# Half-row products of three pairs side by side, and output products ahead of two pairs, in a fused attention and feed-forward kernel

## The chip, the cores and the metric

The kernel runs on one core of a Trainium2 chip. The metric is the device time of one execution in microseconds (us). A program on one core has its runs called fast unless one is over 1.5% above the fastest of the same kernel; all comparisons of times below are between fast runs. The engines are named as in the profile: PE is TensorE (PEld its weight loads), ACT is ScalarE, DVE is VectorE, SP issues the DMAs.

## The reference, cut to what matters

```python
xn = layernorm(x)                              # x: 1 x 2048 x 448
q, k, v = split(xn @ wqkv)                     # 16 heads of 28
logits = q . k[pos - 2*j], j = 0..7            # window of 8, dilation 2, scaled, masked
s = softmax(logits) @ v[...] @ wo
h = gelu(xn @ w1 + b1)                         # 448 -> 1792
g = silu(h @ w2 + b2)                          # 1792 -> 448
out = x + s * g
```

The depth of the first products is 448 = 3 x 128 + 64. The last 64 rows, the "rest", fill half of the TensorE array, so the rests of two products run side by side in its two halves: a pass of two rests takes 0.22 us, as one full product does. The passage of TensorE from full rows to rests, or back, is called a crossing below.

## The kernel before

The sequence is handled in four blocks of 512 positions. Each block has a feed-forward stage with seven pairs of 128-wide tiles (`k` = 0 to 6), and then (but for the last block) units of attention, each with scores `S`, exponentials `E` and value product `psO`. PSUM has two pools: psA with two tiles of two banks each (tag "A"), shared by the scores and most pairs, and psB with four one-bank tiles, for everything else. The kernel fixes the order of the instructions on each engine itself (`manual_schedule`).

```python
def ffn1_tiles(k):
    if k in (0, 3):
        return [psB.tile([P, CH], F32, name="ps_h", tag="B") for _ in range(2)]
    ps = psA.tile([P, 2, CH], F32, name="ps_h", tag="A")
    return [ps[:, i, :] for i in range(2)]
# ffn1_full: per half three 128-row products; ffn1_rest: two 64-row products side by side
def ffn1(c, k, even):
    ps = ffn1_tiles(k)
    if even: ffn1_full(c, k, ps, True);  ffn1_rest(c, k, ps, False)
    else:    ffn1_rest(c, k, ps, True);  ffn1_full(c, k, ps, False)
    return ps

def feed_forward_1(c, ps, wos):
    nc.scalar.preload_act_table_set(SET_GELU)
    gelu(0, ps)
    for k in range(1, MT // 2):
        if (c, k) in ((0, 6), (1, 4), (2, 4)):
            qk_pair(c + 1, 0, True, DD)                # a q/k pair of the next block
        odd = k in {0: (1, 3, 5, 6), 3: (1, 3, 5)}.get(c, (1, 3, 4, 6))
        ps = ffn1(c, k, not odd)
        gelu(k, ps)
        # ... norm statistics behind pairs 1 and 3
        if k in ((3, 5, 6) if c == 3 else (4,)):
            # ... wo_job: four products with wo into psB, gated by g, added to x
        if c and k in (3, 5):
            silu_job(4 * (c - 1) + k - 3)              # tanh on ScalarE, gate g on VectorE
            silu_job(4 * (c - 1) + k - 2)
    nc.scalar.preload_act_table_set(SET_EXP)
```

Pairs with the rest last and pairs with the rest first alternate, so rests already lie in twos.

The softmax here doesn't subtract the row's maximum and nothing guards it: scores larger than these inputs give would overflow.

Of the kernel before, what the change touches and what calls it, by code (L numbers as in the profile page):

```python
# [16 lines left out]
P = 128  # L17
NT = S // P
NC = 4
# [14 lines left out]
def kernel(  # L34
# [58 lines left out]
    def xt(t):  # L93
        return x_sb[t // 4][:, t % 4, :]
# [99 lines left out]
    def qk_full(c, g, ps, first, copies):  # L194
        for w in range(2):
            for kt in range(3):
                nc.tensor.matmul(ps[w][:, :], wqk[:, kt, 16 * w + 4 * g:16 * w + 4 * g + 4, :],  # L197
                                 xnT[:, kt, LEAD + c * CH:LEAD + (c + 1) * CH],
                                 start=(first and kt == 0), stop=(not first and kt == 2))
            if not first:  # L200
                qk_put(c, g, w, ps, copies)

    def qk_rest(c, g, ps, first, copies):

        for w in range(2):
            r = slice(64 * w, 64 * w + 64)
            nc.tensor.matmul(ps[w][:, :], wqk[r, 3, 16 * w + 4 * g:16 * w + 4 * g + 4, :],  # L207
                             xnT[r, 3, LEAD + c * CH:LEAD + (c + 1) * CH], start=first, stop=not first)
        if not first:
            for w in range(2):  # L210
                qk_put(c, g, w, ps, copies)

# [3 lines left out]
    def qk_pair(c, g, even, copies):  # L216

        ps = [psB.tile([P, CH], F32, name="ps_qk", tag="B") for _ in range(2)]
        for f in ((qk_full, qk_rest), (qk_rest, qk_full))[not even]:
            f(c, g, ps, f is (qk_full, qk_rest)[not even], copies)  # L220
# [3 lines left out]
    def v_mm(b):  # L224
        ps = psB.tile([P, D], F32, name="ps_v", tag="B")
        o = LEAD + QB * b - 7
        for kt in range(KT):
            nc.tensor.matmul(ps[:, :], xnT[:, kt, o:o + P], wv[:, kt, :],  # L228
                             start=(kt == 0), stop=(kt == KT - 1))
        return ps  # L230
# [8 lines left out]
    def ffn1_tiles(k):  # L239
        if k in (0, 3):  # L240
            return [psB.tile([P, CH], F32, name="ps_h", tag="B") for _ in range(2)]
        ps = psA.tile([P, 2, CH], F32, name="ps_h", tag="A")
        return [ps[:, i, :] for i in range(2)]

    def ffn1_full(c, k, ps, first):
        for i in range(2):
            m = 2 * k + i
            for kt in range(3):
                nc.tensor.matmul(ps[i][:, :], w1[:, kt, m * P:(m + 1) * P],  # L249
                                 xnT[:, kt, LEAD + c * CH:LEAD + (c + 1) * CH],  # L250
                                 start=(first and kt == 0), stop=(not first and kt == 2))

    def ffn1_rest(c, k, ps, first):

        for i in range(2):
            m = 2 * k + i
            r = slice(64 * i, 64 * i + 64)
            nc.tensor.matmul(ps[i][:, :], w1[r, 3, m * P:(m + 1) * P],  # L258
                             xnT[r, 3, LEAD + c * CH:LEAD + (c + 1) * CH], start=first, stop=not first)

    def gelu(k, ps):
        for i in range(2):
            m = 2 * k + i
            nc.scalar.activation(hT[:, m, :], ps[i][:, :], ACT.Gelu_apprx_tanh, bias=b1f[:, m:m + 1])  # L264

    def ffn1(c, k, even):

        ps = ffn1_tiles(k)
        if even:
            ffn1_full(c, k, ps, True)  # L270
            ffn1_rest(c, k, ps, False)
        else:
            ffn1_rest(c, k, ps, True)
            ffn1_full(c, k, ps, False)
        return ps
# [59 lines left out]
    def wo_put(t, ps, cs=slice(0, D)):  # L335
        sg = work.tile([P, D], BF16, name="sg", tag="sg", bufs=3)
        nc.vector.scalar_tensor_tensor(out=sg[:, cs], in0=ps[:, 0:cs.stop - cs.start], scalar=0.5, in1=g_sb[t % NG][:, cs],  # L337
                                       op0=ALU.mult, op1=ALU.mult)
        o_t = work.tile([P, D], BF16, name="o_t", tag="o_t", bufs=3)
        nc.vector.tensor_tensor(out=o_t[:, cs], in0=xt(t)[:, cs], in1=sg[:, cs], op=ALU.add)  # L340
        nc.sync.dma_start(dram_rows(out_par, t, 1)[:, 0, cs], o_t[:, cs])
# [49 lines left out]
    def feed_forward_1(c, ps, wos):  # L391

        nc.scalar.preload_act_table_set(SET_GELU)
        gelu(0, ps)
        for k in range(1, MT // 2):
            if (c, k) in ((0, 6), (1, 4), (2, 4)):

                qk_pair(c + 1, 0, True, DD)
            odd = k in {0: (1, 3, 5, 6), 3: (1, 3, 5)}.get(c, (1, 3, 4, 6))
            ps = ffn1(c, k, not odd)  # L400
            gelu(k, ps)
            if c + 2 < NC and k in (1, 3):
                for t in range(4 * c + 7 + k, 4 * c + 9 + k):
                    ln_stats(t)
            if k in ((3, 5, 6) if c == 3 else (4,)):
                for _ in range(4 if c == 2 else 2):
                    if wos:
                        wo_job(wos.pop(0))
            if c and k in (3, 5):
                silu_job(4 * (c - 1) + k - 3)  # L410
                silu_job(4 * (c - 1) + k - 2)
        nc.scalar.preload_act_table_set(SET_EXP)


    with tc.manual_schedule(engines={ENG.PE, ENG.Activation, ENG.DVE, ENG.Pool, ENG.SP}):
        nc.scalar.preload_act_table_set(SET_EXP)
        busy(9)
# [16 lines left out]
        v_put(0, v0)  # L434
        ln_apply(2)
        pT.append(ln_tr(2))
        v1 = v_mm(1)
        ln_put(2, pT[2])
        v_put(1, v1)
# [3 lines left out]
        ln_put(3, pT[3])  # L443
        v_put(2, v2)
        v_job(3)
        pb = psB.tile([P, MT], BF16, name="pb", tag="B")
        nc.tensor.transpose(pb[:, :], b1r[:, :], ident[0:MT, 0:MT])
# [4 lines left out]
        late_constants()  # L452
        nc.vector.tensor_copy(b1f[:], pb[:, :])
        for g in range(4):
            qk_pair(0, g, g % 2 == 0, DA)
            if g == 3:
                ln_stats(7)
                ln_rstd(4, 4)
            else:
                ln_stats(4 + g)  # L460
        ps = ffn1(0, 0, True)
        for t in range(4, 8):
            ln_apply(t)
            ln_dma(t)
        late_loads()

        units = iter(range(NB))
        for c in range(3):
            feed_forward_1(c, ps, [[], [0, 1], [2, 3, 4, 5]][c])
            n = c + 1  # L470
            qk_pair(n, 1, True, DD)
            norm = lambda: None
            vs = iter(range(4 * n, 4 * n + (5 if c == 2 else 4)))
            for i in range(5):
                b = next(units)
                if i == 0:
                    tail = []
                    E = qk_unit(b, lambda: qk_pair(n, 2, False, (nc.vector.tensor_copy, lambda *a: tail.append(a))))
                    if n + 1 < NC:
                        ln_rstd(4 * n + 4, 4)  # L480
                    nc.scalar.copy(*tail[0])
                    qk_pair(n, 3, True, DA)
                else:
                    E = qk_unit(b)
# [70 lines left out]
```

## Time and profile before

| | before |
|---|---|
| time, median | 167.58 us (167.44 to 167.74, 3 runs) |
| span of the profiled run | 165.6 us |
| TensorE busy | 158.9 us, 96% |
| ScalarE busy | 125.9 us, 76% |
| VectorE busy | 112.9 us, 68% |

The prediction below shows the lines to read. A view that it doesn't show is the list of what TensorE waited for, with the total, the number and the longest, in us. Before the change, apart from the start of the kernel, it holds nothing but two short entries without a releaser, which come from lost records:

```profile
PE ps_qk L197 <- issue: 0.2, 1, 0.2
PE ps_h L249 <- issue: 0.2, 1, 0.2
```

Waits inside a merged row (the scores' 0.28 us) don't appear there; they are seen as a row that lasts longer than its like.

### The profile page before, as it was taken

Reading aid. Unit: us, or ns where it says so; the run is one execution under the profiler, and the core shown is the slowest. Engines: PE = TensorE matmul, PEld = TensorE weight load, DVE = VectorE, ACT = ScalarE, POOL = GpSimd, SP = SyncE. Lnnn points to the kernel's source line nnn. Section 1 sums busy time; section 2 is a strip of 40 time slices with the busy share of each in tenths; the row PEclk is TensorE's granted clock in tenths of the full one; section 3 lists DMA queues with packets and bytes.
Section 4 is the critical chain, followed back from the end, with each engine's and each line's share of the span. In section 5 each row is a group of like instructions: output and inputs, shape, how many; then the busy total and the mean of one; then the engine's idle time right before and its main releaser. Section 6 shows DMA issues by size and latency. Waiting matters only on the chain.

```text
span 165.6 us, 3242 instructions
## 1 busy us (share of the span) xinstructions
PE 158.9 (96%) x1290; PEld 71.8 (43%) x1301; DVE 112.9 (68%) x256; ACT 125.9 (76%) x198; POOL 4.5 (3%) x16
## 2 busy tenths in 40 slices
PE   6899999999999999999999999999999999999990
PEld 2343333345554334445554334335555334445570
DVE  5967890497888638687888308877777507678893
ACT  3773698598887795998887795698888698698830
POOL 7002000000000000000000000000000000000000
PEclk9999999999999999999999999999999999999999
DMA  5999995520111100100211100300000002020011
GB/s 134 302 306 267 325 190 93 164 44 4 32 36 32 32 0 4 55 0 0 36 32 32 36 0 0 112 1 4 0 4 0 0 0 60 31 83 0 4 55 55
DMA packets 15963, 10.62 MB, mean 64 GB/s; under 512 B 7500, under 2 KB 15948, under 8 KB 15948
## 3 DMA queue, kind: packets, MB, share of 16 engines
q1 hardware_dynamic: 15660, 10.18, 24.0%
q10 hardware_dynamic: 288, 0.23, 0.5%
q8 instruction: 10, 0.16, 0.4%
q14 instruction: 5, 0.04, 0.1%
HBM read 7.00 MB, written 1.84 MB: 53 GB/s over the span
## 4 chain that ended last, share of the span: by engine, by line
PE 83%; ACT 7%; DVE 5%; DMA 2%; issue 1%; DVEq 0%
PE ps_y L281 23%; PE ps_h L249 21%; PE ps_qk L197 11%; PE ps_v L228 8%; PE ps_s L331 6%; PE ps_h L258 4%; PE S L355 3%; PE psO L370 3%; ACT hT L264 3%; PE ps_qk L207 3%; DMA x<-in_A_x_dram 2%; ACT th L310 1%; DVE sg L337 1%; DVE st L161 1%; ACT L509 1%
## 5 line engine op out<-in xcount | busy, mean ns | idle before, releaser
L264 ACT ACTIVATE hT<-ps_h,b1f 128x512 bf16<-128x512 f32 x56 | 34.1, 695 | 10.1 <-PE ps_h L258 7.3
L249 PE MATMUL ps_h<-xnT,w 128*128 128x512 bf16 x161 | 39.3, 380 | 0.5 <-issue 0.2
L281 PE MATMUL ps_y<-w,hT 128*128 128x448 bf16 x196 | 39.5, 353 | 0.0
L361 ACT ACTIVATE E<-S 128x976 bf16<-128x976 f32 x34 | 31.6, 983 | 2.1 <-PE S L355 0.8
L281 PEld LDWEIGHTS <-hT 128*128 128x128 bf16 x196 | 18.0, 98 | 16.7
L249 PEld LDWEIGHTS <-w 128*128 128x128 bf16 x168 | 15.0, 98 | 22.1 <-issue 6.4
L363 DVE TENSOR_TENSOR E<-E,mk_gen 128x976 bf16<-128x976 bf16 x30 | 20.0, 666 | 6.7 <-ACT E L361 6.5
L197 PE MATMUL ps_qk<-xnT,wqk 128*128 128x512 bf16 x92 | 22.2, 380 | 0.3 <-issue 0.2
L379 DVE TENSOR_TENSOR oT<-psO,den 128x484 bf16<-128x484 f32 (+1 forms) x17 | 11.3, 662 | 10.1 <-ACT den L378 10.1
L214 DVE CAST qT<-ps_qk 128x512 bf16<-128x512 f32 x16 | 11.0, 687 | 9.5 <-PE ps_qk L207 8.4
L228 PE MATMUL ps_v<-wv,xnT 128*128 128x448 bf16 x68 | 15.7, 353 | 0.1
L311 DVE SCALAR_TENSOR_TENSOR g<-th,y 128x448 bf16<-128x448 bf16 x13 | 7.6, 621 | 10.8 <-ACT th L310 10.8
L337 DVE SCALAR_TENSOR_TENSOR sg<-ps_s,g 128x448 bf16<-128x448 f32 (+2 forms) x17 | 10.1, 592 | 7.0 <-PE ps_s L331 6.9
L233 ACT CAST vw<-ps_v 128x448 bf16<-128x448 f32 x17 | 9.1, 533 | 6.9 <-PE ps_v L228 6.8
L197 PEld LDWEIGHTS <-wqk 128*128 128x128 bf16 x96 | 8.9, 98 | 11.5 <-issue 1.8
L331 PE MATMUL ps_s<-wo,oT 128*128 128x448 bf16 (+2 forms) x68 | 13.4, 342 | 0.0
L377 ACT ACTIVATE den<-den 128x484 f32<-128x484 f32 (+1 forms) x17 | 10.3, 605 | 4.0 <-DVE den L374 4.0
L374 DVE STREAM_SHUFFLE den<-psO 128x484 f32<-128x484 f32 (+1 forms) x17 | 11.7, 695 | 0.0
L378 ACT ACTIVATE den<-den 128x484 f32<-128x484 f32 (+1 forms) x17 | 10.3, 606 | 0.5
L161 DVE BATCH_NORM_STATS2 st<-x 128x6 f32<-128x448 bf16 x16 | 9.8, 610 | 0.9 <-DMA x<-in_A_x_dram 0.8
L331 PEld LDWEIGHTS <-oT 128*128 128x128 bf16 x68 | 6.4, 98 | 5.9 <-issue 0.2
L228 PEld LDWEIGHTS <-xnT 128*128 128x128 bf16 x68 | 6.3, 98 | 6.0 <-ACT xnT L181 0.6
(71 smaller groups left out, 139.8 us busy)
## 6 DMA issues: line engine op xcount, KB each, us to landing
out_dram<-o_t SPq DMA_DIRECT2D x15, 112.0 KB
w<-in_B_w_dram SPq DMA_DIRECT2D x1, 1568.0 KB
x<-in_A_x_dram SPq DMA_DIRECT2D x3, 448.0 KB
w<-in_B_w_dram SPq DMA_DIRECT2D x2, 672.0 KB
wraw<-in_A_wqkv_dram SPq DMA_DIRECT2D x1, 672.0 KB
w<-in_B_w_dram SPq DMA_DIRECT2D x4, 112.0 KB
wo<-in_A_wo_dram SPq DMA_DIRECT2D x16, 24.5 KB
wv<-in_A_wqkv_dram SPq DMA_DIRECT2D x1, 336.0 KB
```

What stands on the lines that cost most here:

```text
L161: nc.vector.bn_stats(out=st[:], in_=xt(t))
L197: nc.tensor.matmul(ps[w][:, :], wqk[:, kt, 16 * w + 4 * g:16 * w + 4 * g + 4, :], xnT[:, kt, LEAD + c * CH:LEAD + (c + 1) * CH], start=(fi ...
L228: nc.tensor.matmul(ps[:, :], xnT[:, kt, o:o + P], wv[:, kt, :], start=(kt == 0), stop=(kt == KT - 1))
L249: nc.tensor.matmul(ps[i][:, :], w1[:, kt, m * P:(m + 1) * P], xnT[:, kt, LEAD + c * CH:LEAD + (c + 1) * CH], start=(first and kt == 0), st ...
L264: nc.scalar.activation(hT[:, m, :], ps[i][:, :], ACT.Gelu_apprx_tanh, bias=b1f[:, m:m + 1])
L281: nc.tensor.matmul(ps[:, :], hT[:, m, tt * P:(tt + 1) * P], w2[:, m, :], start=(m == 0), stop=(m == MT - 1))
L331: nc.tensor.matmul(ps[:, 0:n], oT[:, g, t * P:(t + 1) * P], wo[:, g, cs], start=(g == 0), stop=(g == 3))
L337: nc.vector.scalar_tensor_tensor(out=sg[:, cs], in0=ps[:, 0:cs.stop - cs.start], scalar=0.5, in1=g_sb[t % NG][:, cs], op0=ALU.mult, op1=AL ...
L361: nc.scalar.activation(ev, Sp[p2][:, :, :, 0:QW], ACT.Exp, scale=SCALE)
L363: nc.vector.tensor_tensor(out=ev, in0=ev, in1=mkb, op=ALU.mult)
L374: nc.vector.stream_shuffle(den[:, :, 0:n], psO[:, :, 0:n], [0] * 32)
L379: nc.vector.tensor_tensor(out=oT[:, :, QB * b:QB * b + n], in0=psO[:, :, 0:n], in1=den[:, :, 0:n], op=ALU.mult)
```

## The change

The intent: fewer passages of TensorE between full and half rows, by putting the rests of up to three pairs into one run; a prologue where ScalarE's copies of value products no longer stand before those of the transposed input; and a last row tile that is added and sent in one piece. To have pair 3 and a q/k pair in one run, the output products now come directly behind them, ahead of pairs 4 and 5.

```diff
+    def group(*jobs):
+        for job in jobs:
+            job.alloc()
+        jobs[0].full(True)
+        jobs[0].rest(False)
+        for job in jobs[1:]:
+            job.rest(True)
+        jobs[0].done(True)
+        for job in jobs[1:]:
+            job.full(False)
+            job.done(False)
...
+        t = 4 * (c - 1)
+        p = [FF1(c, 0, ahead=gelus), FF1(c, 1, then=stats(4 * c + 8)), FF1(c, 2, then=silus(t) if c < 3 else lambda: None),
+             FF1(c, 3, then=stats(4 * c + 10) if c < 3 else silus(t)), FF1(c, 4), FF1(c, 5, then=silus(t + 2)),
+             FF1(c, 6, then=lambda: nc.scalar.preload_act_table_set(SET_EXP))]
+        group(*p[0:3])
+        if c == 3:
+            # ... pairs 3+4, two output products, pairs 5+6, four output products
+        elif c:
+            group(p[3], QK(c + 1, 0, DD))
+            wo_jobs(4)
+            group(*p[4:6])
+            group(p[6], *last)
+        else:
+            # ... pairs 3+4, pairs 5+6, then two q/k pairs with the first scores
...
-        v1 = v_mm(1)
+        v1 = v_mm(1, psA)
         ln_put(2, pT[2])
-        v_put(1, v1)
+        v_put(0, v0)
...
-        wo_put(15, s15, pieces[0])
+        wo_gate(15, s15, pieces[0], sg)
         s15 = wo_mm(15, pieces[1])
         silu_psum(15, y15, pieces[1])
-        wo_put(15, s15, pieces[1])
+        wo_gate(15, s15, pieces[1], sg)
+        wo_sum(15, sg)
```

The scores of a block's first unit lie between the full products of a q/k pair, the "score pair" below: VectorE copies its q half out of PSUM, and ScalarE copies its k half behind the exponentials of these scores.

In the second and third block the first two tanh (`silus(t)`) move from behind pair 3 to behind pair 2, since the output products need their gates.

More of the change, by code (lines that the diff above doesn't have):

```diff
@@ L192, in qk_weights @@
                               bass.AP(src.tensor, src.offset, [list(src.ap[0]), [DH, H], [1, 32]]))
-    def qk_full(c, g, ps, first, copies):
-        for w in range(2):
-            for kt in range(3):
-                nc.tensor.matmul(ps[w][:, :], wqk[:, kt, 16 * w + 4 * g:16 * w + 4 * g + 4, :],
-                                 xnT[:, kt, LEAD + c * CH:LEAD + (c + 1) * CH],
-                                 start=(first and kt == 0), stop=(not first and kt == 2))
-            if not first:
-                qk_put(c, g, w, ps, copies)
@@ L203, in qk_rest, with __init__, alloc, full @@
-    def qk_rest(c, g, ps, first, copies):
-        for w in range(2):
-            r = slice(64 * w, 64 * w + 64)
-            nc.tensor.matmul(ps[w][:, :], wqk[r, 3, 16 * w + 4 * g:16 * w + 4 * g + 4, :],
-                             xnT[r, 3, LEAD + c * CH:LEAD + (c + 1) * CH], start=first, stop=not first)
-        if not first:
-            for w in range(2):
-                qk_put(c, g, w, ps, copies)
     def qk_put(c, g, w, ps, copies):
         copies[w]((qT, kT)[w][:, g, LEAD + c * CH:LEAD + (c + 1) * CH], ps[w][:, :])
-    def qk_pair(c, g, even, copies):
-        ps = [psB.tile([P, CH], F32, name="ps_qk", tag="B") for _ in range(2)]
-        for f in ((qk_full, qk_rest), (qk_rest, qk_full))[not even]:
-            f(c, g, ps, f is (qk_full, qk_rest)[not even], copies)
+    class QK:
+        def __init__(self, c, g, copies):
+            self.c, self.g, self.copies = c, g, copies
+        def alloc(self):
+            self.ps = [psB.tile([P, CH], F32, name="ps_qk", tag="B") for _ in range(2)]
+        def full(self, first):
+            c, g = self.c, self.g
+            for w in range(2):
+                for kt in range(3):
+                    nc.tensor.matmul(self.ps[w][:, :], wqk[:, kt, 16 * w + 4 * g:16 * w + 4 * g + 4, :],
+                                     xnT[:, kt, LEAD + c * CH:LEAD + (c + 1) * CH],
+                                     start=(first and kt == 0), stop=(not first and kt == 2))
+                if not first:
+                    qk_put(c, g, w, self.ps, self.copies)
+        def rest(self, first):
+            c, g = self.c, self.g
+            for w in range(2):
+                r = slice(64 * w, 64 * w + 64)
+                nc.tensor.matmul(self.ps[w][:, :], wqk[r, 3, 16 * w + 4 * g:16 * w + 4 * g + 4, :],
+                                 xnT[r, 3, LEAD + c * CH:LEAD + (c + 1) * CH], start=first, stop=not first)
+        def done(self, first):
+            if first:
+                for w in range(2):
+                    qk_put(self.c, self.g, w, self.ps, self.copies)
@@ L222, with v_mm @@
+    def group(*jobs):
[9 more added lines that the diff above has]
+            job.done(False)
     DA, DD = (nc.vector.tensor_copy, nc.scalar.copy), (nc.vector.tensor_copy, nc.vector.tensor_copy)
-    def v_mm(b):
-        ps = psB.tile([P, D], F32, name="ps_v", tag="B")
+    def v_mm(b, pool=psB):
+        ps = pool.tile([P, D], F32, name="ps_v", tag="B" if pool is psB else "A")
@@ L236, in v_job @@
         v_put(b, v_mm(b))
-    def ffn1_tiles(k):
-        if k in (0, 3):
-            return [psB.tile([P, CH], F32, name="ps_h", tag="B") for _ in range(2)]
-        ps = psA.tile([P, 2, CH], F32, name="ps_h", tag="A")
-        return [ps[:, i, :] for i in range(2)]
-    def ffn1_full(c, k, ps, first):
-        for i in range(2):
-            m = 2 * k + i
-            for kt in range(3):
-                nc.tensor.matmul(ps[i][:, :], w1[:, kt, m * P:(m + 1) * P],
-                                 xnT[:, kt, LEAD + c * CH:LEAD + (c + 1) * CH],
-                                 start=(first and kt == 0), stop=(not first and kt == 2))
@@ L253, in ffn1_rest, with __init__, alloc, full @@
-    def ffn1_rest(c, k, ps, first):
-        for i in range(2):
-            m = 2 * k + i
-            r = slice(64 * i, 64 * i + 64)
-            nc.tensor.matmul(ps[i][:, :], w1[r, 3, m * P:(m + 1) * P],
-                             xnT[r, 3, LEAD + c * CH:LEAD + (c + 1) * CH], start=first, stop=not first)
-    def gelu(k, ps):
-        for i in range(2):
-            m = 2 * k + i
-            nc.scalar.activation(hT[:, m, :], ps[i][:, :], ACT.Gelu_apprx_tanh, bias=b1f[:, m:m + 1])
-    def ffn1(c, k, even):
-        ps = ffn1_tiles(k)
-        if even:
-            ffn1_full(c, k, ps, True)
-            ffn1_rest(c, k, ps, False)
-        else:
-            ffn1_rest(c, k, ps, True)
-            ffn1_full(c, k, ps, False)
-        return ps
+    class FF1:
+        def __init__(self, c, k, ahead=lambda: None, then=lambda: None):
+            self.c, self.k, self.ahead, self.then = c, k, ahead, then
+        def alloc(self):
+            if self.k in (0, 3):
+                self.ps = [psB.tile([P, CH], F32, name="ps_h", tag="B") for _ in range(2)]
+            else:
+                ps = psA.tile([P, 2, CH], F32, name="ps_h", tag="A")
+                self.ps = [ps[:, i, :] for i in range(2)]
+        def full(self, first):
+            for i in range(2):
+                m = 2 * self.k + i
+                for kt in range(3):
+                    nc.tensor.matmul(self.ps[i][:, :], w1[:, kt, m * P:(m + 1) * P],
+                                     xnT[:, kt, LEAD + self.c * CH:LEAD + (self.c + 1) * CH],
+                                     start=(first and kt == 0), stop=(not first and kt == 2))
+        def rest(self, first):
+            for i in range(2):
+                m = 2 * self.k + i
+                r = slice(64 * i, 64 * i + 64)
+                nc.tensor.matmul(self.ps[i][:, :], w1[r, 3, m * P:(m + 1) * P],
+                                 xnT[r, 3, LEAD + self.c * CH:LEAD + (self.c + 1) * CH],
+                                 start=first, stop=not first)
+        def done(self, first):
+            self.ahead()
+            for i in range(2):
+                m = 2 * self.k + i
+                nc.scalar.activation(hT[:, m, :], self.ps[i][:, :], ACT.Gelu_apprx_tanh, bias=b1f[:, m:m + 1])
+            self.then()
@@ L333, in wo_mm, with wo_gate, wo_sum, wo_put @@
         return ps
-    def wo_put(t, ps, cs=slice(0, D)):
-        sg = work.tile([P, D], BF16, name="sg", tag="sg", bufs=3)
-        nc.vector.scalar_tensor_tensor(out=sg[:, cs], in0=ps[:, 0:cs.stop - cs.start], scalar=0.5, in1=g_sb[t % NG][:, cs],
-                                       op0=ALU.mult, op1=ALU.mult)
-        o_t = work.tile([P, D], BF16, name="o_t", tag="o_t", bufs=3)
-        nc.vector.tensor_tensor(out=o_t[:, cs], in0=xt(t)[:, cs], in1=sg[:, cs], op=ALU.add)
-        nc.sync.dma_start(dram_rows(out_par, t, 1)[:, 0, cs], o_t[:, cs])
+    def wo_gate(t, ps, cs, sg):
+        nc.vector.scalar_tensor_tensor(out=sg[:, cs], in0=ps[:, 0:cs.stop - cs.start], scalar=0.5,
+                                       in1=g_sb[t % NG][:, cs], op0=ALU.mult, op1=ALU.mult)
+    def wo_sum(t, sg):
+        o_t = work.tile([P, D], BF16, name="o_t", tag="o_t", bufs=3)
+        nc.vector.tensor_tensor(out=o_t[:], in0=xt(t), in1=sg[:], op=ALU.add)
+        nc.sync.dma_start(dram_rows(out_par, t, 1)[:, 0, :], o_t[:])
+    def wo_put(t, ps):
+        sg = work.tile([P, D], BF16, name="sg", tag="sg", bufs=3)
+        wo_gate(t, ps, slice(0, D), sg)
+        wo_sum(t, sg)
     def wo_job(t):
@@ L389, in busy, with feed_forward_1, gelus, stats @@
             nc.tensor.matmul(ps[:, :], wz[:, 0:P], wz[:, :], start=True, stop=True)
-    def feed_forward_1(c, ps, wos):
-        nc.scalar.preload_act_table_set(SET_GELU)
-        gelu(0, ps)
-        for k in range(1, MT // 2):
-            if (c, k) in ((0, 6), (1, 4), (2, 4)):
-                qk_pair(c + 1, 0, True, DD)
-            odd = k in {0: (1, 3, 5, 6), 3: (1, 3, 5)}.get(c, (1, 3, 4, 6))
-            ps = ffn1(c, k, not odd)
-            gelu(k, ps)
-            if c + 2 < NC and k in (1, 3):
-                for t in range(4 * c + 7 + k, 4 * c + 9 + k):
-                    ln_stats(t)
-            if k in ((3, 5, 6) if c == 3 else (4,)):
-                for _ in range(4 if c == 2 else 2):
-                    if wos:
-                        wo_job(wos.pop(0))
-            if c and k in (3, 5):
-                silu_job(4 * (c - 1) + k - 3)
-                silu_job(4 * (c - 1) + k - 2)
-        nc.scalar.preload_act_table_set(SET_EXP)
+    def feed_forward_1(c, ahead, wos, last=()):
+        def gelus():
+            ahead()
+            nc.scalar.preload_act_table_set(SET_GELU)
+        def stats(t):
+            def f():
+                if c + 2 < NC:
+                    ln_stats(t)
+                    ln_stats(t + 1)
+            return f
+        def silus(t):
+            def f():
+                if c:
+                    silu_job(t)
+                    silu_job(t + 1)
+            return f
+        def wo_jobs(n):
+            for _ in range(n):
+                if wos:
+                    wo_job(wos.pop(0))
+        t = 4 * (c - 1)
[4 more added lines that the diff above has]
+        if c == 3:
+            group(*p[3:5])
+            wo_jobs(2)
+            group(*p[5:7])
+            wo_jobs(4)
+        elif c:
+            group(p[3], QK(c + 1, 0, DD))
+            wo_jobs(4)
+            group(*p[4:6])
+            group(p[6], *last)
+        else:
+            group(*p[3:5])
+            group(*p[5:7])
+            group(QK(1, 0, DD), last[0])
@@ L415 @@
     with tc.manual_schedule(engines={ENG.PE, ENG.Activation, ENG.DVE, ENG.Pool, ENG.SP}):
         nc.scalar.preload_act_table_set(SET_EXP)
-        busy(9)
+        busy(10)
         ln_stats(0)
@@ L433 @@
         ln_rstd(3, 1)
-        v_put(0, v0)
         ln_apply(2)
         pT.append(ln_tr(2))
-        v1 = v_mm(1)
+        v1 = v_mm(1, psA)
         ln_put(2, pT[2])
-        v_put(1, v1)
+        v_put(0, v0)
         ln_apply(3)
@@ L443 @@
         ln_put(3, pT[3])
+        v_put(1, v1)
+        v3 = v_mm(3, psA)
         v_put(2, v2)
-        v_job(3)
-        pb = psB.tile([P, MT], BF16, name="pb", tag="B")
-        nc.tensor.transpose(pb[:, :], b1r[:, :], ident[0:MT, 0:MT])
+        v_put(3, v3)
         for which in range(2):
@@ L452 @@
         late_constants()
+        group(QK(0, 0, DA), QK(0, 1, DA))
+        pb = psB.tile([P, MT], BF16, name="pb", tag="B")
+        nc.tensor.transpose(pb[:, :], b1r[:, :], ident[0:MT, 0:MT])
         nc.vector.tensor_copy(b1f[:], pb[:, :])
-        for g in range(4):
-            qk_pair(0, g, g % 2 == 0, DA)
-            if g == 3:
-                ln_stats(7)
-                ln_rstd(4, 4)
-            else:
-                ln_stats(4 + g)
-        ps = ffn1(0, 0, True)
-        for t in range(4, 8):
-            ln_apply(t)
-            ln_dma(t)
@@ L465, with first_norm, __init__, full @@
-        late_loads()
+        ln_stats(4)
+        ln_stats(5)
+        group(QK(0, 2, DA), QK(0, 3, DA))
+        ln_stats(6)
+        ln_stats(7)
+        ln_rstd(4, 4)
+        def first_norm():
+            for t in range(4, 8):
+                ln_apply(t)
+                ln_dma(t)
+            late_loads()
+        class Scores:
+            def __init__(self, qk, b):
+                self.qk, self.b, self.late = qk, b, []
+                qk.copies = (nc.vector.tensor_copy, lambda *a: self.late.append(a))
+                self.alloc, self.rest, self.done = qk.alloc, qk.rest, qk.done
+            def full(self, first):
+                self.E = qk_unit(self.b, lambda: self.qk.full(first))
@@ L467 @@
         units = iter(range(NB))
+        norm = first_norm
         for c in range(3):
-            feed_forward_1(c, ps, [[], [0, 1], [2, 3, 4, 5]][c])
             n = c + 1
-            qk_pair(n, 1, True, DD)
-            norm = lambda: None
+            b = next(units)
+            sc = Scores(QK(n, 2 if c else 1, None), b)
+            feed_forward_1(c, norm, [[], [0, 1], [2, 3, 4, 5]][c], (QK(n, 1, DD), sc) if c else (sc,))
+            if n + 1 < NC:
+                ln_rstd(4 * n + 4, 4)
+            nc.scalar.copy(*sc.late[0])
+            group(*(QK(n, g, DA) for g in ((3,) if c else (2, 3))))
+            norm = av_unit(b, sc.E)
@@ L473 @@
             vs = iter(range(4 * n, 4 * n + (5 if c == 2 else 4)))
-            for i in range(5):
+            for i in range(1, 5):
                 b = next(units)
-                if i == 0:
-                    tail = []
-                    E = qk_unit(b, lambda: qk_pair(n, 2, False, (nc.vector.tensor_copy, lambda *a: tail.append(a))))
-                    if n + 1 < NC:
-                        ln_rstd(4 * n + 4, 4)
-                    nc.scalar.copy(*tail[0])
-                    qk_pair(n, 3, True, DA)
-                else:
-                    E = qk_unit(b)
-                    norm()
-                    ffn2_job(4 * c + i - 1)
-                    v_job(next(vs))
-                    if n + 1 < NC:
-                        ln_apply(4 * n + 3 + i)
-                        ln_dma(4 * n + 3 + i)
+                E = qk_unit(b)
+                norm()
+                ffn2_job(4 * c + i - 1)
+                v_job(next(vs))
+                if n + 1 < NC:
+                    ln_apply(4 * n + 3 + i)
+                    ln_dma(4 * n + 3 + i)
@@ L491 @@
                 norm = av_unit(b, E)
-            norm()
             for b in vs:
                 v_job(b)
-            ps = ffn1(n, 0, True)
-        feed_forward_1(3, ps, [6, 7, 8, 9, 10, 11])
+        feed_forward_1(3, norm, [6, 7, 8, 9, 10, 11])
         E15 = qk_unit(15)
@@ L521 @@
         s15 = wo_mm(15, pieces[0])
+        sg = work.tile([P, D], BF16, name="sg", tag="sg", bufs=3)
         y15 = ffn2_biased(psA, "A", 15, pieces[1])
-        wo_put(15, s15, pieces[0])
+        wo_gate(15, s15, pieces[0], sg)
         s15 = wo_mm(15, pieces[1])
         silu_psum(15, y15, pieces[1])
-        wo_put(15, s15, pieces[1])
+        wo_gate(15, s15, pieces[1], sg)
+        wo_sum(15, sg)
 _INS = ['A_x', 'A_wqkv', 'A_wo', 'B_x', 'B_w1', 'B_b1', 'B_w2', 'B_b2']
```

## The prediction

> **What bounds the kernel now.** I read the busy shares first, then the chain that ended last, then the TensorE and ScalarE timelines of one block, then the closing microseconds.
>
> ```profile
> PE 158.9 (96%) x1290; PEld 71.8 (43%) x1301; DVE 112.9 (68%) x256; ACT 125.9 (76%) x198; POOL 4.5 (3%) x16
> ...
> PE 83%; ACT 7%; DVE 5%; DMA 2%; issue 1%; DVEq 0%
> ```
>
> TensorE is busy 96% of the 165.6 us span and carries 83% of the chain. Time can only be won by taking work, gaps or waits out of its stream, and any new wait in that stream is lost in full. The second feed-forward block (from 53.12 us) shows both; columns are start and duration in us, then engine, line, operation and count.
>
> ```profile
> 53.12 1.47 PE L249 MATMUL ps_h<-xnT,w 128*128 128x512 bf16 x5
> 54.53 0.60 PE L258 MATMUL ps_h<-xnT,w 64*128 64x512 bf16 x4
> 55.06 2.76 PE L249 MATMUL ps_h<-xnT,w 128*128 128x512 bf16 x12
> 57.76 0.61 PE L258 MATMUL ps_h<-xnT,w 64*128 64x512 bf16 x4
> 58.30 1.47 PE L249 MATMUL ps_h<-xnT,w 128*128 128x512 bf16 x6
> 59.60 1.46 PE L197 MATMUL ps_qk<-xnT,wqk 128*128 128x512 bf16 x6
> ...
> 67.58 1.46 PE L197 MATMUL ps_qk<-xnT,wqk 128*128 128x512 bf16 x6
> 68.97 0.39 PE L207 MATMUL ps_qk<-xnT,wqk 64*128 64x512 bf16 x2
> 69.30 0.67 PE L355 MATMUL S<-qT,kT 28*128 28x122 bf16 x16
> ```
>
> Read the starts. Six full matmuls with another full one behind take 59.60-58.30 = 1.30 us, 0.216 each. Six with a 64-row rest behind take 68.97-67.58 = 1.39. So **a crossing into the rests costs 0.10 us**. Four rests (two side by side, twice) take 58.30-57.76 = 0.54: two passes of 0.22 and 0.10 for the way out. A crossing either way is thus 0.10. (x5 or x11 is a lost record, not a gap.) The score group at 69.30 lasts 0.67 against 0.39 in later units: it waits 0.28. The chain names the cause:
>
> ```profile
> 66.17 1.27 ACT hT L264 x2
> 67.44 0.93 ACT th L310 x2
> 68.37 1.17 ACT hT L264 x2
> 69.53 0.04 issue
> 69.58 0.39 PE S L355 x14
> ...
> 73.31 0.54 PE psO L370 x16
> ```
>
> ScalarE's gelu of pair 5, two tanh and the gelu of pair 6 hold the score banks. The value product at 73.31 takes 0.54 instead of 0.33: 0.20 more, for the exponentials behind a table load. The third block (from 90.45) repeats both waits. The last view to read is ScalarE's line of time in the same block:
>
> ```profile
> 54.77 0.61 ACT L377 ACTIVATE den<-den 128x484 f32<-128x484 f32 x1 [1.34 <-DVE den L374]
> 55.41 0.61 ACT L378 ACTIVATE den<-den 128x484 f32<-128x484 f32 x1
> 56.03 1.28 ACT L393 ACT_TABLE_LOAD   x1
> 57.33 4.74 ACT L264 ACTIVATE hT<-ps_h,b1f 128x512 bf16<-128x512 f32 x8
> 61.90 1.09 ACT L310 ACTIVATE th<-y 128x448 bf16<-128x448 f32 x2
> ```
>
> The first gelu starts 4.20 us after the block's first matmul, since the last unit's norm and the table load are ahead of it. The eight gelus take 61.90-57.33 = 4.57, or 0.57 each. ScalarE is then some three pairs behind TensorE; today nothing on TensorE needs it that early.
>
> **What the Trainium skill says.** "TensorEngine Tiling (Array Packing)", Key Properties: changing the tiling mode, not just the tile, drains TensorE. It gives no figure; the trace agrees, with 0.10 us. "TensorE: Matmul & The Clock Gate", The mechanism (Part 3): matmuls start and end in program order, so one that waits for a bank holds all later ones; the 0.28 us at the scores agrees, as the q/k matmuls behind stood still. "ScalarE: Activation LUTs", What ACT_TABLE_LOAD costs: about 1.28 us and a drain of about 1.38. The 1.28 is in the trace, the drain isn't: the gelu follows 0.02 us after the load. I use 1.28.
>
> **The change part by part.** It removes no product. It moves rests together, changes TensorE's order, adds one warm-up matmul and takes one addition and one transfer from the end.
>
> *Crossings*, counted from the order in the code, ten fewer of 0.10:
> - First block: the four q/k pairs stay in twos (2 runs of rests); seven pairs go as 3+2+2; the two q/k pairs before the scores share a run that leads into the scores. 18 crossings become 16.
> - Second and third: before, four runs, one on each side of the scores and one before the value product, 14. After: 3, 2 and 2, then pair 6 with two q/k pairs into the scores, then the last q/k pair: 11.
> - Last: four runs become three, 8 to 6.
>
> That is 2+3+3+2 = 10, **-1.0 us**, all on TensorE and so on the path.
>
> *Prologue.* ScalarE's copy of value product 0 no longer stands before the transposed tile 2, nor copy 1 before tile 3. The third copy of tile 3 waited for today ends at 10.30, and value product 3 starts at 10.36. In the new order I place it at 9.51 + 0.59 = 10.10: tile 2's copy from 8.53 (0.55 to the next), value copy from 9.08 (0.43 to the next). **-0.20.** The bias transpose moves behind two q/k pairs at the same cost. The tenth warm-up ends at about 5.53, before the transpose at 5.55: nothing.
>
> *Output products ahead of pairs 4 and 5.* Here I see the cost. psB has four banks. Pair 3 takes two and the q/k pair beside it the other two; the output products come directly behind and need one of them. Counting from the block's first matmul, on TensorE: six full 1.30, crossing 0.10, three rest passes 0.67, crossing 0.10 (2.16 with rounding), pairs 1 and 2 2.60 (4.76), pair 3 1.30 (6.05), crossing, two passes, crossing 0.64 (6.69), q/k 1.30: **output products reached at 7.99**. On ScalarE: first gelu at 4.20 as now, six gelus 3.43 (7.63), then the two tanh, which now stand ahead of pair 3: 0.93 (8.56), and the first gelu of pair 3 0.69: **its bank free at 9.25**, the second at 9.83. With 0.05 for the signal the wait is 9.30-7.99 = **1.31 us, new, in the second block and again in the third**. The q/k banks can't help: their VectorE copies are behind the two gating products, which wait for tanh and end near 9.4. The first block has no output products, and the last has pairs 3 and 4 together, so its first two find pair 0's banks, long free.
>
> *What that gives back.* The second block in full, after 9.30: eight output products 1.50, pairs 4 and 5 with their crossings 3.23 (14.04), pair 6 1.30, three passes with crossings 0.86 (16.19), q/k 1.30, crossing: scores at 17.59. ScalarE by then: pair 5's gelus end at 14.9, tanh 0.93, pair 6's end at 17.13. So the score wait of 0.28 goes. Scores with the way out 0.33, two q/k pairs 2.59, crossing, pass, crossing: value product at 20.92. The exponentials (table load from 17.15, 0.99 and 0.89, then 0.67 for the mask) end at 21.01, so 0.11 of wait is left. Value products get going at 21.03; today at 73.24+0.20-53.12 = 20.32. **The second block loses 0.7.** The third has 1.50 more of output products in both kernels and loses 0.7 too.
>
> *End.* After the gate of the first piece (161.40, 0.50) today's 0.33 us addition goes, so the second piece is gated 0.29 earlier; but the final addition is 0.39 instead of 0.22: the last transfer starts 0.12 earlier. It then carries 112 KB, not 28: in the trace the rows of such a transfer take 0.50 us to move, those of the last small one 0.25. **+0.1.**
>
> Sum: first block and prologue -0.2-0.2, second +0.7, third +0.7, last -0.2, end +0.1: **+0.9 us, so 168.5.** (The crossings of blocks two and three are inside their +0.7.)
>
> **Rivals.**
> 1. *The wait for pair 3's banks doesn't come.* Then only crossings, prologue and the two score waits count: 168.5-2.6 = 165.9. For it: the change reads as if tuned, and the wait rests on four banks and on tanh ahead of gelu. Against it: all four banks are held by pair 3 and q/k whichever the allocator picks, and today's profile has ScalarE's first gelu at 4.20 in both blocks.
> 2. *ScalarE becomes the bound of the block.* Rests at the end of pairs 4 and 5, instead of ahead, complete both halves together, so gelus start later, and the exponentials slip behind the value product. I left 0.11 of wait there; 0.4 in two blocks would give 169.3. Against it: ScalarE is idle some 2 us while the output products wait and run.
> 3. *The gain is hidden at the end*, since the closing chain is ScalarE and VectorE. Against: that chain hangs on the last feed-forward products at 152.3, so it moves with TensorE.
>
> **Range and chances.** 168.5, eight times in ten within 167.2 and 169.3: the low end has half of each new wait missing, the high end has rival 2. Even rival 1 is 1% off, so 2% either way (3.35 us) needs something that I haven't seen: faster 0.01, same 0.97, slower 0.02.
>
> **What would show it.** The profile after should show: 11 and 16 crossings per block as counted; an idle or stretched first output product of about 1.3 us in the second and third block, released by gelu (hT), at 8.0 us from the block's start; score groups at 0.39; the value product about 0.1 stretched; value product 3 near 10.15; one 112 KB transfer last. A first output product without a wait would make the prediction wrong, towards 166; a wait at pair 4 or at the value product, towards 169 and over.

## The result, and the profile after

The changed kernel took 169.42 us (median of 5, 169.38 to 169.97) against 167.49 us (167.22 to 167.74, 5 runs). The ratio is 1.0121, with a 95% interval of 1.0101 to 1.0140. Ratios here are the mean time of one kernel's fast runs over that of the other's of the same rounds, so not quite the ratio of the medians. It is within 2%, slower, and just over the range that was predicted: +1.9 us where +0.9 was forecast.

TensorE has less to do and a longer span; ScalarE's share of the chain has grown from 7% to 23%:

```profile
PE 157.9 (94%) x1291; PEld 71.7 (43%) x1302; DVE 112.0 (67%) x254; ACT 125.9 (75%) x199; POOL 4.5 (3%) x16
...
PE 63%; ACT 23%; DVE 9%; DMA 2%; issue 1%; DVEq 0%
```

The list of TensorE's waits now names who holds it:

```profile
PE ps_s L346 <- ACT hT L289: 2.4, 2, 1.2
...
PE psO L391 <- DVE E L384: 0.6, 2, 0.3
```

The second block on TensorE (it starts at 53.44):

```profile
53.44 1.47 PE L273 MATMUL ps_h<-xnT,w 128*128 128x512 bf16 x5
54.84 0.82 PE L281 MATMUL ps_h<-xnT,w 64*128 64x512 bf16 x6
55.60 4.06 PE L273 MATMUL ps_h<-xnT,w 128*128 128x512 bf16 x18
...
60.13 1.47 PE L209 MATMUL ps_qk<-xnT,wqk 128*128 128x512 bf16 x6
62.78 1.67 PE L346 MATMUL ps_s<-wo,oT 128*128 128x448 bf16 x8 [1.19 <-ACT hT L289]
...
71.07 0.45 PE L376 MATMUL S<-qT,kT 28*128 28x122 bf16 x16
...
74.47 0.23 PE L391 MATMUL psO<-E,vw 128*32 128x122 bf16 x2
75.01 0.39 PE L391 MATMUL psO<-E,vw 128*32 128x122 bf16 x14 [0.30 <-DVE E L384]
```

Six rests stand in one run. The q/k product is through at 61.43 (60.13 and six products), but the first output product starts at 62.78: 1.35 us of wait. (The profile's 1.19 counts from the modelled end of the last matmul.) The value product breaks after two matmuls. Sixteen of them take 0.33 us when nothing holds them, some 0.02 each, so the next start, at 75.01 rather than at about 74.50, is 0.5 us late. ScalarE meanwhile:

```profile
57.64 3.58 ACT L289 ACTIVATE hT<-ps_h,b1f 128x512 bf16<-128x512 f32 x6
61.08 1.07 ACT L325 ACTIVATE th<-y 128x448 bf16<-128x448 f32 x2
62.01 1.30 ACT L289 ACTIVATE hT<-ps_h,b1f 128x512 bf16<-128x512 f32 x2
66.11 1.27 ACT L289 ACTIVATE hT<-ps_h,b1f 128x512 bf16<-128x512 f32 x2 [2.81 <-PE ps_h L281]
67.73 1.27 ACT L289 ACTIVATE hT<-ps_h,b1f 128x512 bf16<-128x512 f32 x2 [0.35 <-PE ps_h L273]
```

Pair 3's gelus stand behind six gelus and two tanh, and the first is over at 62.73 (it lasts 0.72); the output product starts 0.05 later. Then ScalarE idles 2.81 us, until pair 4 comes, and 0.35 more ahead of pair 5.

To see where all the time went, I cut both spans at the same events. A block runs from its first feed-forward product to the second score group behind it, the last block to its first.

| stretch, us | before | after | forecast for the difference | measured difference |
|---|---|---|---|---|
| first input tile there | 3.63 | 3.98 | none | +0.35 |
| from there to the first feed-forward product | 14.18 | 13.96 | -0.2 | -0.22 |
| first block | 18.65 | 18.83 | -0.2 | +0.18 |
| second block | 20.65 | 21.89 | +0.7 | +1.24 |
| third block | 22.18 | 23.39 | +0.7 | +1.21 |
| last block | 16.06 | 15.85 | -0.2 | -0.21 |
| last value products to the end | 13.31 | 13.40 | +0.1 | +0.09 |
| everything else | 56.95 | 56.95 | 0 | 0 |

The arrival of the first input tile isn't the change's doing: in the twelve traces it lies between 3.30 and 3.98 us, with no order by kernel. Without it the stretches add up to +2.3. The medians say +1.9, and the ratio +2.0. The profiled run of the changed kernel took 169.97 us, the other four 169.38 to 169.43; a different arrival in the runs compared is enough for the rest, but I have no trace of those runs to show it. Three stretches are off the forecast: the first three blocks, by 0.4 to 0.5 each.

### The profile page after: what moved, and what is told of

Same layout as the page of the kernel before. It is cut to its first block, busy times and chain, and to the rows that moved or that the text cites. A ratio compares the mean times of both kernels' runs of the same rounds, so it can differ in the third digit from the quotient of the medians.

```text
span 168.2 us, 3237 instructions
## 1 busy us (share of the span) xinstructions
PE 157.9 (94%) x1291; PEld 71.7 (43%) x1302; DVE 112.0 (67%) x254; ACT 125.9 (75%) x199; POOL 4.5 (3%) x16
## 4 chain that ended last, share of the span: by engine, by line
PE 63%; ACT 23%; DVE 9%; DMA 2%; issue 1%; DVEq 0%
PE ps_y L296 20%; PE ps_h L273 14%; ACT hT L289 8%; PE ps_v L246 7%; PE ps_qk L209 6%; PE ps_s L346 6%; ACT E L382 4%; PE S L376 3%; PE ps_h L281 3%; PE psO L391 3%; ACT th L325 3%; ACT den L399 2%; ACT den L398 2%; DMA x<-in_A_x_dram 2%; PE ps_qk L219 2%; ACT L439 2%
## 5 line engine op out<-in xcount | busy, mean ns | idle before, releaser
L273 PE MATMUL ps_h<-xnT,w 128*128 128x512 bf16 x161 | 38.6, 380 | 0.4
L195 ACT CAST kT<-ps_qk 128x512 bf16<-128x512 f32 x8 | 4.7, 590 | 5.8 <-PE ps_qk L209 3.4
```

The lines of the kernel that those rows point to most:

```text
L195: copies[w]((qT, kT)[w][:, g, LEAD + c * CH:LEAD + (c + 1) * CH], ps[w][:, :])
L273: nc.tensor.matmul(self.ps[i][:, :], w1[:, kt, m * P:(m + 1) * P], xnT[:, kt, LEAD + self.c * CH:LEAD + (self.c + 1) * CH], start=(first a ...
```

## The experiments

All kernels gave correct results. The kernel before ran in each session, at a median of 167.12 us (first four runs), 167.51 (next four) and 167.56 (last two). A total of one session is therefore compared with the kernel before in that session (the ratios), and the stretches are compared from trace to trace. My theory was that three separate waits explain everything: the output products for pair 3's banks (A), the value product for late exponentials, and a wait in the rests at the end of the first block, which the trace shows and the prediction had not: four rests there take 1.00 us where 0.60 is usual. The main rival was that the runs of three rests, with six sums open at once, cost something themselves.

**Output products behind pairs 4 and 5.**

```diff
             group(p[3], QK(c + 1, 0, DD))
-            wo_jobs(4)
             group(*p[4:6])
+            wo_jobs(4)
+            silus(t + 2)()
             group(p[6], *last)
             # ... and pair 5 no longer issues silus(t + 2) in these two blocks
```

> Output products of blocks two and three moved behind pairs 4 and 5 (the later pair of tanh and their gating products moved behind them in program order, so that they do not hold up VectorE). Theory A (the 1.35 us gap in each block is the output product waiting for pair 3's PSUM banks, which ScalarE frees late): both gaps vanish, and because pairs 4 and 5 reach ScalarE earlier, the wait of the value product for the exponentials falls from 0.53 to about 0.1. Block length from its first matmul to the second score group falls from 21.9 to about 20.1 us in block two; total about 165.7 us, 1% under the kernel before. Rival B (the order is harmless and the loss is in the three rests side by side, six accumulations open at once): the time stays near 169.4.

Measured: 165.78 us, ratio 0.9916 (0.9903 to 0.9929). The second block takes 20.07 us and the third 21.59, each 1.8 under the changed kernel. In the second block no row waits before the output products, and the value product's row lasts 0.52, where one that nothing holds lasts 0.40:

```profile
63.07 1.47 PE L273 MATMUL ps_h<-xnT,w 128*128 128x512 bf16 x6
64.38 1.68 PE L346 MATMUL ps_s<-wo,oT 128*128 128x448 bf16 x8
...
72.78 0.52 PE L391 MATMUL psO<-E,vw 128*32 128x122 bf16 x16
```

The runs of three rests are all still there and the time is below the kernel before, so the rival falls. This edit moves two things at once (output products and the later gates), so it shows the place of the loss and not yet its mechanism.

**First two tanh behind pair 3.**

```diff
-FF1(c, 2, then=silus(t) if c < 3 else lambda: None),
-FF1(c, 3, then=stats(4 * c + 10) if c < 3 else silus(t)),
+FF1(c, 2),
+FF1(c, 3, then=both(silus(t), stats(4 * c + 10)) if c < 3 else silus(t)),
```

> First two tanh of blocks two and three moved from behind pair 2 to behind pair 3. Theory A, bank by bank: pair 3's gelus come 0.93 us earlier, so the wait at the first output product falls from 1.35 to about 0.4 in both blocks. In block three a third output product is needed, whose bank is held by the q/k copy on VectorE, which now stands behind gating products that wait for the later tanh: a new wait of about 1.4 us there. Net: block two 0.95 shorter, block three about 0.4 longer, total about 168.9. If it is not bank by bank but ScalarE's whole backlog that holds the output products, nothing changes (169.4).

Measured: 168.83 us, ratio 1.0100. The second block falls from 21.89 to 20.95 us, the third rises from 23.39 to 23.79, as expected bank by bank. In the third block TensorE now waits twice, first some 0.4 us for a gelu, then some 1.3 for a q/k copy, counted as the 1.35 above:

```profile
97.08 1.47 PE L209 MATMUL ps_qk<-xnT,wqk 128*128 128x512 bf16 x6
98.80 1.67 PE L346 MATMUL ps_s<-wo,oT 128*128 128x448 bf16 x8 [0.25 <-ACT hT L289]
101.64 1.67 PE L346 MATMUL ps_s<-wo,oT 128*128 128x448 bf16 x8 [1.17 <-DVE qT L195]
```

This settles A: the output products wait for whichever reader still holds the psB bank that comes next.

**The k half of block one's score pair copied at once.**

```diff
-qk.copies = (nc.vector.tensor_copy, lambda *a: self.late.append(a))
+qk.copies = (nc.vector.tensor_copy,
+             (lambda *a: self.late.append(a)) if wait else nc.vector.tensor_copy)   # wait: not in block one
```

> In block one only, the k half of the pair that carries the first scores is copied by VectorE at once instead of by ScalarE behind the exponentials. Theory C (the 0.40 us gap in the rests of the last two q/k pairs of block one is the wait for this bank): the gap goes, the value product starts 0.40 earlier, about 169.0. Rival: the rests there wait for something else (weights, xnT), and the gap stays.

Measured: 169.01 us, ratio 1.0110. The first block falls from 18.83 to 18.43, the others stay. The row of four rests ahead of the value product is 1.00 in the changed kernel and normal here:

```profile
34.11 1.00 PE L219 MATMUL ps_qk<-xnT,wqk 64*128 64x512 bf16 x4
```

```profile
33.66 0.60 PE L219 MATMUL ps_qk<-xnT,wqk 64*128 64x512 bf16 x4
```

So the last q/k pair of block one waited for the bank of the score pair's k half, whose copy stands on ScalarE behind the exponentials. By the code, the group brings this about: the rests of the last two q/k pairs, now in one run, write all four banks of psB.

**Each gelu behind its own half.** In the changed kernel pair 5's first gelu started at 14.28 us of the second block; I had counted on some 13.8, when pair 4's gelus are done and the products of pair 5's first half are there. The edit issues it between the halves:

```diff
                     nc.tensor.matmul(self.ps[i][:, :], w1[:, kt, m * P:(m + 1) * P], ...)
+                if not first:
+                    self.gelu(i)
                 # ... and done() issues the gelus only of the pair that had its rests last
```

> Each gelu of a pair whose rests came first is issued right behind the three matmuls of its own half, instead of behind all six. Theory D (the step of the prediction that failed is the assumption that the first half's gelu starts when its own products are ready, where in fact it waits for the pair's last matmul): the first gelu of pair 5 starts about 0.5 us earlier, exponentials and value product likewise, the value product's wait falls from 0.53 to about 0.1 in blocks two and three and the gap in block one's rests from 0.40 to about 0; the 1.35 waits stay. About 168.1. Rival E (the two banks of a tile are guarded as one): the second half's matmuls then wait for the first half's gelu, 0.6 us per such pair, and the time rises above 172.

Measured: 193.28 us (median of the three fast runs; three more were slow), ratio 1.1539. My theory's expectation failed and the rival's came true, only more so. The profiled run is a slow one, with a mean granted clock of 0.945 where the fast ones had 0.969 to 0.979, so I take no sizes from it, but it names the wait:

```profile
63.12 0.82 PE L273 MATMUL ps_h<-xnT,w 128*128 128x512 bf16 x3
67.06 1.50 PE L273 MATMUL ps_h<-xnT,w 128*128 128x512 bf16 x6 [3.12 <-ACT hT L289]
```

After three matmuls of pair 1's first half the second half waits for the first half's gelu, although it writes another bank. And that gelu is behind the norm, the table load and pair 0 on ScalarE, so the wait is far over the 0.6 that I had allowed. The two banks are one tile of the program, and the program guards the tile as one. Then a gelu issued behind both halves must wait for the last product in the tile, whichever half it reads.

**Pair 5 in two tiles of its own**, to test that reading without moving any instruction:

```diff
-            if self.k in (0, 3):
+            if self.k in ((0, 3, 5) if self.c in (1, 2) else (0, 3)):
                 self.ps = [psB.tile([P, CH], F32, name="ps_h", tag="B") for _ in range(2)]
```

> The changed kernel with one thing else: in blocks two and three pair 5 gets two separate one-bank tiles (from psB) instead of one two-bank tile; order and products stay. Theory D2 (a gelu reads half of a two-bank tile and waits for the last product written anywhere in that tile, which is why the first half's gelu came late, and why the run with gelu by half stalled TensorE): pair 5's first gelu no longer waits for the pair's last matmul and starts when pair 4's gelus end, about 13.8 us from the block's first matmul instead of 14.28; the value product's wait falls from 0.53 to about 0.1 in both blocks; total about 168.5. Rival (the gelu waits because of the order in which the matmuls were issued, whatever the tile): the start stays at 14.28, the wait at 0.53, the total at 169.4.

Measured: 168.53 us, ratio 1.0062; the second and the third block are 0.47 and 0.46 shorter. ScalarE goes from pair 4 straight into pair 5 (four gelus in one row; the third is pair 5's first and starts at 66.70, or 13.83 us from the block's start at 52.87):

```profile
65.65 2.76 PE L273 MATMUL ps_h<-xnT,w 128*128 128x512 bf16 x12
...
65.54 2.42 ACT L289 ACTIVATE hT<-ps_h,b1f 128x512 bf16<-128x512 f32 x4 [2.81 <-PE ps_h L281]
67.83 1.06 ACT L325 ACTIVATE th<-y 128x448 bf16<-128x448 f32 x2
```

The pair's last product starts only at about 66.73 (65.65 and five products), so the gelu no longer waits for it. In the changed kernel the gelu starts at 67.73, where the pair's six products end at 67.69 (they begin at 66.22 and such a row lasts 1.47). The value product's row is 0.52 again, some 0.1 over a free one. The edit also moves pair 5 out of psA, so other banks come free at other times; but no instruction is moved, and the gelu's start, 0.45 us earlier, is nearly all of the 0.47. The guard by tile is the cause of the late exponentials in these two blocks.

**The first three pairs as two and one**, on the kernel with the output products behind:

```diff
-        group(*p[0:3])
+        group(*p[0:2])
+        group(p[2])
```

> On the kernel with the output products behind pairs 4 and 5, the first group of three pairs in each of the four blocks is split into two and one: two more crossings per block, eight in all, same products. If a crossing costs TensorE 0.097 us wherever it stands: 8 x 0.097 = 0.78 us longer than the 165.78 of the unsplit one, about 166.55. If crossings are hidden in waits for ScalarE: no longer than 0.4.

Measured: 166.67 us, ratio 0.9952. Each of the four blocks is 0.21 or 0.22 longer than unsplit (19.04, 20.29, 21.80, 16.06 against 18.83, 20.07, 21.59, 15.85), so a crossing is 0.105 us in all of them. In the traces this kernel has just as many crossings in each block as the kernel before, so this is what the grouping saves: 0.85 us. The grouping as such does what it was made for.

**Both repairs together.**

> Both repairs together: output products behind pairs 4 and 5, and block one's k half copied at once by VectorE. If the two waits are separate they add: 165.78 - 0.40 = about 165.4, which is some 1.0 to 1.2% under the kernel before. If the wait at the rests was only slack of a later wait: 165.8.

Measured: 165.50 us, ratio 0.9879 (0.9859 to 0.9900). The blocks are 18.43, 20.07, 21.59 and 15.85: the repairs add. This version beats both kernels.

**The prologue alone, on the kernel before**: value products 1 and 3 to psA, and the order of copies as in the diff.

> The kernel before with only the prologue of the change (value products 1 and 3 in the other banks, ScalarE's copies of value products behind the next transposed tile; nine warm-up matmuls as before). From the arrival of the first input tile to the first q/k product: 7.70 us in the kernel before; expected 0.20 less, 7.50. The arrival itself differs from run to run by some 0.3, so the total, about 0.2 under the kernel before, may be unclear.

Measured: 7.48 us from the input tile to the first q/k product against 7.69. The total, 167.17 us with a ratio of 0.9982 (0.9960 to 1.0005), is unclear, as expected.

**The closing sum alone, on the kernel before**: one addition and one transfer.

> The kernel before with only the closing sum in one piece (one 448-wide addition and one 112 KB transfer instead of 336 + 112 wide). From the start of the last two value products to the end of the span: 13.31 us in the kernel before; the prediction's working gives 0.1 more (addition starts 0.29 earlier, lasts 0.17 longer, transfer takes 0.25 longer); in the trace of the whole change it was 13.35. Total within 0.15 of the kernel before, no verdict expected from the totals; the trace decides.

Measured: 13.39 us from the last value products to the end against 13.31 (and 13.40 in the whole change; the text above has 13.35 from a rounded span); total 167.77 us, ratio 1.0021 (1.0003 to 1.0039). One piece costs 0.08.

**Both repairs, closing sum in two pieces again.**

> Both repairs (output products behind pairs 4 and 5, k half copied at once) with the closing sum in two pieces as in the kernel before. If one piece costs 0.04 to 0.12 us, this is that much faster than the 165.5 with one piece; if one piece wins, slower. From the last two value products to the end 13.31 if the two-piece ending is as in the kernel before.

Measured: 165.34 us, ratio 0.9877 (0.9858 to 0.9897); the end is back to 13.31. By the trace it is the best version, by the totals alone it can't be told from the one above.

## Why the prediction was wrong

Most steps hold. *Crossings*: the cost of 0.10 holds, the count doesn't. In the traces each block has two fewer, so they are eight and not ten. The prediction's "11" for the second and third block should be 12: it leaves out the way from the scores back to full rows, which the 14 before it includes. The +0.7 was summed row by row and isn't touched by this. The last block, where nothing waits, is 0.21 shorter for its two, and the split groups, which bring all eight back, cost 0.85. *Prologue*: -0.2 forecast, -0.22 measured. *Output products ahead of pairs 4 and 5*: reached at 7.99, bank free at 9.25, wait of 1.31 forecast; 7.99, 9.29 and 1.35 measured (7.99, 9.28 and 1.34 in the third block), and the bank-by-bank run confirms the mechanism. *End*: +0.1 forecast, +0.09 measured. The score wait of 0.28 nearly went: the row is 0.45 instead of 0.67.

The step that failed is the one under "What that gives back": "pair 5's gelus end at 14.9, tanh 0.93, pair 6's end at 17.13", and from it "so 0.11 of wait is left". I had let the first gelu of pair 5 start as soon as its own half was ready and pair 4's gelus were done. Measured, pair 5's gelus end at 15.55 and pair 6's at 17.64, and the value product waits 0.5 instead of 0.11. The reason is that a pair's two banks are one tile, and a gelu waits for the last product in that tile. The kernel before could have told me. In its first block pair 6 has its rests first; ScalarE is idle for 1.97 us before its gelus:

```profile
29.43 1.47 PE L249 MATMUL ps_h<-xnT,w 128*128 128x512 bf16 x6
30.94 1.27 ACT L264 ACTIVATE hT<-ps_h,b1f 128x512 bf16<-128x512 f32 x2 [1.97 <-PE ps_h L249]
```

The six full products end at 30.90, and the first half's three were through 0.65 us earlier, yet the first gelu starts at 30.94.

In the first block the step that failed is another: the prediction counted two crossings and nothing else ("-0.2") and kept no account of psB's banks. The wait of 0.4 for the score pair's k copy came instead; the run with the immediate copy takes it out. Its size fits the same lateness of gelus: pair 6's first gelu in the changed kernel starts 0.46 us later than pair 5's gelus and its own half would allow, and the table load, the exponentials and the k copy follow behind it. That is worked out from the trace; no run split pair 6's tile there.

In sum: 0.4 in the first block, and 0.5 each in the second and third. That is 1.4 us, and +0.9 with it would be +2.3, what the traces show. Rival 2 had named the direction ("exponentials slip behind the value product") and its size in two blocks, but not the reason: it blamed rests at the end of pairs 4 and 5, and pair 5 still has its rests ahead. It also overlooked block one. Rival 1, no wait at the banks, was wrong, and so was rival 3: the 0.21 that the last block saved was not lost behind it, where the end differs by 0.09.

## What to carry to other kernels

When TensorE's order is changed to save its own 0.1 us gaps, walk through the queue of the engine that empties PSUM at the same time: a product moved forward meets banks that are not yet read, and eight saved crossings of 0.1 were lost to two waits of 1.35. Work out readiness by the tile that the program guards, not by the bank that an instruction touches; where a reader should start on half of a pair, give the halves tiles of their own. And put what needs a fresh bank behind work whose bank has long been free: the same grouping with the output products two pairs later was 1.2% faster than before, with the one late copy repaired too.

## What the Trainium skill lacked or had wrong

- "TensorEngine Tiling (Array Packing)", Key Properties, says that a change of the tiling mode drains TensorE, without a figure. Here each passage between 128 and 64 rows costs 0.10 us; eight added ones cost 0.85 in all.
- "ScalarE: Activation LUTs", What ACT_TABLE_LOAD costs, adds a drain of about 1.38 us to each load of another set. No trace here shows it on either side of the load: in the kernel before, the load starts 0.01 us after the activation ahead of it, takes 1.28 us, and the first gelu starts 0.02 us later.
- No page that I read says that a program may guard a PSUM tile of two banks as one. Here pair 5's first gelu started 0.45 us earlier when the pair had two tiles (13.83 against 14.28), and a gelu between the halves stalled TensorE (193.28 us).
